# Sending the first two units of a feed-forward layer through half of the weights at a time

## The chip, the cores and the metric

The kernel runs on one core of a Trainium2 chip. The time is the device time of one execution in microseconds (us). Engines: TensorE (PE, with its weight loads as PEld), VectorE (DVE), ScalarE (ACT), GpSimd (POOL) and SyncE (SP), whose queue issues all DMAs here.

## What is computed

Causal attention over 8 batches, 8 heads, 576 tokens and 64 columns a head, blended with a read from a memory matrix, then a feed-forward layer over all 4608 tokens. Shortened:

```
scores = q @ k.T / 8, causal;  a = softmax(scores);  local = a @ v
q_p = elu(q) + 1
mem_out = (q_p @ M_prev) / (q_p @ z_prev + 1e-6)
attn = sigmoid(beta) * mem_out + (1 - sigmoid(beta)) * local      # [8, 8, 576, 64]
x = attn, heads side by side                                      # [4608, 512]
h = x @ w_in                                                      # w_in  [512, 2048], float64
out = (h * sigmoid(h)) @ w_out                                    # w_out [2048, 512], float64
```

## The kernel before

**Attention** goes head by head, 64 in all, batch by batch. `scores` makes one head's probabilities: transposes on VectorE (L221), score products on TensorE (L250), the row minimum on VectorE (L252), exponentials on ScalarE (L254), scaling on GpSimd (L304). `values` transposes the probabilities, multiplies by the values and writes the head's 64 columns into `xt` in two parts, the first 256 tokens and the other 320 (L425 or L430). The first ten heads ("whole") use plain float32 products; the later ones split each operand into a high and a low part in the faster format F32R. Two heads overlap: the scores of head n stand between the values of head n-1.

**Preparation of the weights.** Each of the 2048 ff columns belongs to one of 16 chunks of 128; a chunk has a tile of `w_in` ("i") and one of `w_out` ("o"), so 32 in all. They come as float64. `load_weight` (L138) brings a tile in as words, and `split_weight` makes float32 of it and then a high and a low part: three instructions on VectorE (L152, L154, L159), three on ScalarE (L150, L158, L161) and two on GpSimd (L156, L162). Twenty of the 32 stay in SBUF; twelve ("FLOW") are stored to DRAM and fetched again for each unit (L485).

**The feed-forward layer** works on 18 units of 256 tokens. `split_x` makes the high and low part of a unit's `xt` (L504, L505). A unit needs all eight heads of its batch: units 0 and 1 need heads 0 to 7, unit 2 needs heads 8 to 15. For each of the eight pairs of chunks p there are 24 first products (L552, into `h`), tanh and the blend (L563, L564), the split of g (L567 on ScalarE, L569 on GpSimd, or on VectorE once attention is over), and 12 second products (L532), which add up over all pairs in two PSUM tiles `acc`. The second product of pair p follows the first product of pair p+1. At the end of a unit `acc` is copied with scale 0.5 (L579) and stored (L581).

**Order.** A planner at the end of the function interleaves three generators: one step of attention, then as many weight tiles and product steps as are due. A head has ten steps, since its nine yields are followed by the call that ends it. Preparation is due at `PREP_RATE` = 3 tiles per nine steps, and `PREP_AFTER` = 3 after the first eight heads. Product steps begin when eight heads are done, at step 88; a unit has 17. The first 34 steps come at `FIRST_RATE` = 0.2 units per nine attention steps, later ones at `FFN_RATE` = 0.22. Where a unit's heads are not done, the planner goes on with attention. What attention leaves over runs at the end. The order of the text is a priority: the framework puts the instructions of each engine in order by it, and moves one up when it is ready and the engine would be idle.

Buffers that the parts share: "row" (4: `wy` of the preparation, `th`, `o`), "g" (4: raw weights and g), `xu` (6), one PSUM tile for `h` during attention, two for `acc`.

Of the kernel before, what the change touches and what calls it, by code (L numbers as in the profile page):

```python
# [8 lines left out]
F32 = mybir.dt.float32  # L9
# [3 lines left out]
AF = mybir.ActivationFunctionType  # L13
ALU = mybir.AluOpType
# [14 lines left out]
N_WHOLE = 10  # L29
ROW_BUFS = 4  # L30
W_AHEAD = 2
PREP_RATE = 3.0
PREP_AFTER = 3.0
FFN_RATE = 0.22
FIRST_RATE = 0.2
FIRST_UNITS = 2
W_EARLY = 2

# [2 lines left out]
def memory_attention_then_silu_ffn(ctx, tc, q, k, v, M_prev, z_prev, beta, w_in, w_out, out):  # L41
    nc = tc.nc
    B, H, S, D = q.shape
    NT, DM = out.shape
    DFF = w_in.shape[1]
    P = 128
# [4 lines left out]
    T = 256  # L51
    NU = NT // T
    KD = DM // P
    KF = DFF // P
    NP = KF // 2
# [5 lines left out]
    FLOW = {("i", c) for c in FLOW_IN} | {("o", c) for c in FLOW_OUT}  # L61
# [4 lines left out]
    dram = ctx.enter_context(tc.tile_pool(name="scratch", bufs=1, space=DRAM))  # L66
# [6 lines left out]
    def f(ap):  # L73
        return ap.bitcast(F32)
# [11 lines left out]
        out=mask[:, 3 * P:], in_=mask[:, 3 * P:], pattern=[[-1, P]], base=0, channel_multiplier=1,  # L86
# [54 lines left out]
    def split_weight(kind, c, raw):  # L141
# [24 lines left out]
    ready, anchor = set(), {}  # L166


    order = [
        (kind, 2 * x + j) for p in range(NP + 1) for kind, x in (("i", p), ("o", p - 1))  # L170
        if 0 <= x < NP for j in range(2)]
    loaded = []

    def load_next(n):
# [4 lines left out]
    def preparation():  # L179
        for n, x in enumerate(order):  # L180
            with tc.issue_after(anchor["dve"]):
                split_weight(*x, loaded.pop(0))
            load_next(n + W_AHEAD)
            ready.add(x)
            yield
# [248 lines left out]
    done = [0]  # L434
# [37 lines left out]
                second = values(b, h, made, xt[b, h // 2], n < N_WHOLE)  # L472


    flow_order = [(kind, 2 * p + j) for p in range(NP + 1) for kind, p in (("i", p), ("o", p - 1)) for j in range(2)]
    flow_order = [x for _ in range(NU) for x in flow_order if x in FLOW]
    flowing = []

    def flow():
        if flow_order:  # L480
            while flow_order[0] not in ready:
                yield "prepare"
            x = flow_order.pop(0)
            t = weight_tile(*x)
            nc.sync.dma_start(out=f(t), in_=scratch[x])  # L485
            flowing.append((x, t))

    def fetch(kind, c):
        if (kind, c) not in FLOW:
            return weight[kind, c]  # L490
        x, t = flowing.pop(0)
        assert x == (kind, c)
        return t

    def split_x(u):
        xu = []
        for kk in range(KD):
            t = pool.tile([P, 2, T], F32R, tag="xu", name="xu", bufs=XU_BUFS)
            t0 = u * T
            while t0 < (u + 1) * T:  # L500
                b = t0 // S
                n = min((b + 1) * S, (u + 1) * T) - t0
                src, o = xt[b, kk][:, t0 - b * S:t0 - b * S + n], t0 - u * T
                nc.scalar.copy(t[:, 0, o:o + n], src)  # L504
                nc.vector.tensor_tensor(out=t[:, 1, o:o + n], in0=src, in1=f(t[:, 0, o:o + n]), op=ALU.subtract)  # L505
                t0 += n
            xu.append(t)
        return xu

    def heads_needed(u):  # L510
        return ((u + 1) * T - 1) // S * H + H

    def ffn():
        ahead = None
        for _ in range(FLOW_BUFS):
            yield from flow()
        for u in range(NU):
            while done[0] < heads_needed(u):
                yield "wait"
            xu = ahead or split_x(u)  # L520
            ahead = None
            bank, tag = (ps_s, "s") if done[0] == B * H and u % 2 else (ps_a, "a")
            acc = [bank.tile([P, DM], F32, tag=tag, name="acc") for _ in range(T // P)]

            def second(p, g):
                for c in range(2):
                    w = fetch("o", 2 * p + c)
                    for t in range(T // P):
                        at = slice(t * P, (t + 1) * P)
                        terms = [(g[:, gi, c, at], w[:, wi]) for gi, wi in ((0, 0), (0, 1), (1, 0))]  # L530
                        for n, (ta, tb) in enumerate(terms):
                            nc.tensor.matmul(  # L532
                                acc[t], ta, tb, start=p == 0 and c == 0 and n == 0,
                                stop=p == NP - 1 and c == 1 and n == len(terms) - 1)
                    if ("o", 2 * p + c) in FLOW:
                        yield from flow()

            before = None
            for p in range(NP):
                while not {("i", 2 * p), ("i", 2 * p + 1)} <= ready:  # L540
                    yield "prepare"
                if done[0] == B * H and p % 2:
                    h = ps_t.tile([P, 2, T], F32, tag="t", name="h")
                else:
                    h = ps_h.tile([P, 2, T], F32, tag="h", name="h")
                for c in range(2):
                    w = fetch("i", 2 * p + c)
                    w4 = w.rearrange("p a (k f) -> p a k f", f=P)
                    for kk in range(KD):
                        terms = [(w4[:, wi, kk], xu[kk][:, xi]) for wi, xi in ((0, 0), (0, 1), (1, 0))]  # L550
                        for n, (ta, tb) in enumerate(terms):
                            nc.tensor.matmul(  # L552
                                h[:, c], ta, tb, start=kk == 0 and n == 0,
                                stop=kk == KD - 1 and n == len(terms) - 1)
                    if ("i", 2 * p + c) in FLOW:
                        yield from flow()
                yield
                if before:
                    yield from second(*before)

                h = h.rearrange("p c t -> p (c t)")
                th = pool.tile([P, 2 * T], F32, tag="row", name="th", bufs=ROW_BUFS)
                nc.scalar.activation(th, h, AF.Tanh, scale=0.5)  # L563
                nc.vector.scalar_tensor_tensor(out=th, in0=th, scalar=1.0, in1=h, op0=ALU.add, op1=ALU.mult)  # L564
                g = pool.tile([P, 2, 2, T], F32R, tag="g", name="g", bufs=G_BUFS)
                hi, lo = (g[:, j].rearrange("p c t -> p (c t)") for j in range(2))
                nc.scalar.copy(hi, th)  # L567
                late = nc.vector if done[0] == B * H else nc.gpsimd
                late.tensor_tensor(out=lo, in0=th, in1=f(hi), op=ALU.subtract)  # L569
                while not {("o", 2 * p), ("o", 2 * p + 1)} <= ready:  # L570
                    yield "prepare"
                before = p, g
                if p == NP - 2 and u + 1 < NU and done[0] >= heads_needed(u + 1):
                    ahead = split_x(u + 1)
                yield
            yield from second(*before)
            for t in range(T // P):
                o = pool.tile([P, DM], F32, tag="row", name="o", bufs=ROW_BUFS)
                nc.scalar.activation(o, acc[t], AF.Copy, scale=0.5)  # L579
                r0 = u * T + t * P  # L580
                nc.sync.dma_start(out=out[r0:r0 + P, :], in_=o)  # L581
            yield

    A_STEPS, F_STEPS = 9, 2 * NP + 1
    att, prep, prod = attention(), preparation(), ffn()
    steps, produced, steps_made = 0, 0.0, 0
    going = True
    while going:  # L590
        going = next(att, "end") != "end"
        steps += 1
        started = done[0] >= H
        while going and len(ready) < min(2 * KF, steps * (PREP_AFTER if started else PREP_RATE) / A_STEPS):
            next(prep)
        if started:
            produced += (FFN_RATE if steps_made >= FIRST_UNITS * F_STEPS else FIRST_RATE) * F_STEPS / A_STEPS
        while going and produced >= 1.0:
            said = next(prod, "end")
            if said == "wait":  # L600
                produced = min(produced, 1.0)
                break
            if said == "prepare":
                next(prep)
                continue
            produced -= 1.0
            steps_made += 1
# [28 lines left out]
```

## Time and profile before

| | |
|---|---|
| median of 3 runs | 1315.68 us (1314.75 to 1318.42) |
| the profiled execution | 1315.66 us, span 1313.9 us |
| PE busy / PEld busy | 1266.3 us (96%) / 1084.0 us (83%) |
| DVE / ACT / POOL busy | 898.1 us (68%) / 884.5 us (67%) / 822.9 us (63%) |
| chain that ended last, by engine | PE 73%, DVE 11%, ACT 6% |
| first products L552 | 2592 + 864 matmuls |
| second products L532 | 864 + 864 matmuls |

The profile is one execution. "Busy" is the time in which an engine has an instruction; TensorE's matmuls are pipelined, so a full PE isn't yet PE at its peak, and the weight loads (PEld) show better how densely it works. A row of a table of stretches gives the stretch, its length, then the busy time of each engine with the number of instructions in brackets, the granted clock of TensorE (1.00 is full speed), the busy share of the DMA engines and GB/s. Where the table is asked for one line or tile alone, it has only the columns of the engines that run it. A row of the order of time gives start and duration of an instruction, its engine, line, operation and tiles.

### The profile page before, as it was taken

To read this page: it belongs to the slowest core of one execution; us is meant where nothing else is said; L and a number is where in the kernel's file an instruction comes from. 1 tells how busy PE (TensorE), PEld (TensorE's weight loads), DVE (VectorE), ACT (ScalarE), POOL (GpSimd) and SP (SyncE) were. 2 spreads that over 40 slices of the span, in tenths; PEclk is the share of its full clock that TensorE was granted. 3 is DMA by queue.
4 is the path that set the end of the run, shared out by engine and by line. 5 is a ranking of instruction groups with operands and counts; after the bars stand their busy time and mean duration, and the time that the engine had idled before them with its cause. 6 is when DMAs were issued, how large, how long until landed. Compare 5 with 4: busy or idle time off the path is not lost.

```text
span 1313.9 us, 24653 instructions
## 1 busy us (share of the span) xinstructions
PE 1266.3 (96%) x7858; PEld 1084.0 (83%) x7858; DVE 898.1 (68%) x2472; ACT 884.5 (67%) x2143; POOL 822.9 (63%) x1133
## 2 busy tenths in 40 slices
PE   6988999999999999999999999999999999999998
PEld 2343458888999989998988989899898998999997
DVE  7988875778777777787767777777877775332222
ACT  6777866777787777777777777787878774322222
POOL 6878995777777777777777777767767763000000
PEclk9987779999999999999999999999999999999999
DMA  6766555555455555555555555555545432444444
GB/s 165 188 184 168 162 134 164 144 131 146 125 145 147 138 153 138 150 131 149 137 137 143 145 138 154 137 137 136 158 129 156 123 123 81 145 154 149 152 156 143
DMA packets 302994, 190.39 MB, mean 145 GB/s; under 512 B 258832, under 2 KB 267024, under 8 KB 302864
## 3 DMA queue, kind: packets, MB, share of 16 engines
q1 hardware_dynamic: 302864, 188.82, 51.9%
q8 instruction: 62, 1.02, 0.3%
q14 instruction: 68, 0.56, 0.1%
HBM read 173.02 MB, written 15.73 MB: 144 GB/s over the span
## 4 chain that ended last, share of the span: by engine, by line
PE 73%; DVE 11%; ACT 6%; issue 3%; POOL 3%; DMA 3%; SPq 1%; POOLq 0%; DVEq 0%; ACTq 0%
PE h L552 28%; PE acc L532 25%; PE x L422 7%; PE s L250 5%; PE tp L376 4%; PE tq L351 1%; PE x L414 1%; DVE s L252 1%; DVE wy L159 1%; DVE pl L407 1%; DVE st L290 1%; ACT p L254 1%; POOL p L304 1%; PE s L274 1%; DVE wy L154 1%
## 5 line engine op out<-in xcount | busy, mean ns | idle before, releaser
L552 PE MATMUL h<-xu,wi 128*128 128x256 f32 x2592 | 376.8, 287 | 8.7 <-DVE th L564 6.1
L552 PEld LDWEIGHTS h<-xu,wi 128*128 128x128 f32 x2592 | 343.0, 191 | 24.6 <-DVE th L564 7.8
L532 PE MATMUL acc<-wo,g 128*128 128x512 f32 x864 | 243.0, 398 | 0.0
L532 PE MATMUL acc<-flow,g 128*128 128x512 f32 x864 | 231.0, 394 | 0.5 <-DMA flow<-wo_s 0.5
L304 POOL TENSOR_SCALAR p<-p,st 128x384 f32<-128x384 f32 (+3 forms) x320 | 182.8, 592 | 75.3 <-DVE st L302 72.2
L564 DVE SCALAR_TENSOR_TENSOR th<-th,h 128x512 f32<-128x512 f32 x144 | 98.2, 683 | 143.5 <-ACT th L563 141.7
L532 PEld LDWEIGHTS acc<-flow,g 128*128 128x128 f32 x864 | 158.8, 188 | 33.6 <-DMA flow<-wo_s 1.0
L254 ACT ACTIVATE p<-s,st 128x128 f32<-128x128 f32 (+3 forms) x256 | 134.9, 528 | 69.9 <-DVE st L252 52.8
L569 POOL TENSOR_TENSOR g<-th,g 128x512 fp32r<-128x512 f32 x108 | 140.2, 1298 | 48.7 <-ACT g L567 46.9
L532 PEld LDWEIGHTS acc<-wo,g 128*128 128x128 f32 x864 | 149.1, 189 | 18.9 <-POOL p L304 0.5
L563 ACT ACTIVATE th<-h 128x512 f32<-128x512 f32 x144 | 85.9, 597 | 99.7 <-PE h L552 97.4
L407 DVE TENSOR_TENSOR pl<-tp,ph 128x384 fp32r<-128x384 f32 x216 | 118.5, 551 | 34.6 <-ACT ph L406 31.3
L252 DVE CUSTOM_DVE_ANT_0 s<-s,mask 128x128 f32<-128x128 f32 (+3 forms) x256 | 125.3, 491 | 23.1 <-PE s L250 19.6
L567 ACT CAST g<-th 128x512 fp32r<-128x512 f32 x144 | 89.2, 620 | 53.0 <-DVE th L564 52.1
L376 PE MATMUL tp<-ident,p 128*128 128x128 f32 x640 | 121.8, 291 | 3.2 <-POOL p L304 2.5
L552 PE MATMUL h<-xu,flow 128*128 128x256 f32 x864 | 122.6, 283 | 0.0
L406 ACT CAST ph<-tp 128x384 fp32r<-128x384 f32 x216 | 104.7, 490 | 26.1 <-PE x L422 21.2
L552 PEld LDWEIGHTS h<-xu,flow 128*128 128x128 f32 x864 | 112.8, 191 | 1.9 <-issue 0.3
L376 PEld LDWEIGHTS tp<-ident,p 128*128 128x128 f32 x640 | 82.2, 148 | 28.6 <-POOL p L304 9.0
L422 PE MATMUL x<-pl,vs 128*128 128x256 f32 x324 | 82.1, 308 | 0.9 <-DVE pl L407 0.9
L232 POOL TENSOR_TENSOR kk<-tt,kk 64x576 fp32r<-64x576 f32 x54 | 77.4, 1432 | 5.0 <-ACT kk L230 1.2
L422 PE MATMUL x<-ph,vs 128*128 128x320 f32 (+4 forms) x378 | 78.2, 275 | 1.4 <-POOL vs L316 0.8
(104 smaller groups left out, 2409.5 us busy)
## 6 DMA issues: line engine op xcount, KB each, us to landing
flow<-wo_s SPq DMA_DIRECT2D x144, 512.0 KB, 3.6
flow<-wi_s SPq DMA_DIRECT2D x72, 512.0 KB, 3.8
raw<-in_k SPq DMA_DIRECT2D x128, 72.0 KB, 2.5
raw<-in_q SPq DMA_DIRECT2D x128, 72.0 KB, 2.7
out<-o SPq DMA_DIRECT2D x36, 256.0 KB, 4.2
wraw<-in_moe_w_in SPq DMA_DIRECT2D x16, 512.0 KB, 4.4
qn<-in_q SPq DMA_DIRECT2D x64, 128.0 KB, 2.9
vr<-in_v SPq DMA_DIRECT2D x64, 128.0 KB, 2.5
```

The costliest lines, as they stand in the source:

```text
L252: anchor["dve"] = nc.vector.tensor_tensor_reduce(s, s, mask[:, 3 * P - P * i:], QS, 3.0e38, ALU.add, ALU.min, st[:, i:i + 1]).ins
L254: nc.scalar.activation(pt, s, AF.Exp, bias=st[:, i:i + 1], scale=-1.0, accum_out=st[:, 10 + i:11 + i])
L304: nc.gpsimd.tensor_scalar(pb[x], pb[x], st[:, 15 + x:16 + x], 1.0, op0=ALU.mult, op1=ALU.mult)
L376: nc.tensor.transpose(t[:, o:o + P], pb[i][:, P * j:P * j + P], ident)
L406: nc.scalar.copy(ph[:, 0:o], t[:, 0:o])
L407: nc.vector.tensor_tensor(out=pl[:, 0:cut], in0=t[:, 0:cut], in1=f(ph[:, 0:cut]), op=ALU.subtract)
L422: nc.tensor.matmul(x[0:rows, q0:n], vs[0:n_k, j], part[0:n_k, o:o + n - q0], start=False, stop=last)
L532: nc.tensor.matmul(acc[t], ta, tb, start=p == 0 and c == 0 and n == 0, stop=p == NP - 1 and c == 1 and n == len(terms) - 1)
L552: nc.tensor.matmul(h[:, c], ta, tb, start=kk == 0 and n == 0, stop=kk == KD - 1 and n == len(terms) - 1)
L564: nc.vector.scalar_tensor_tensor(out=th, in0=th, scalar=1.0, in1=h, op0=ALU.add, op1=ALU.mult)
L567: nc.scalar.copy(hi, th)
L569: late.tensor_tensor(out=lo, in0=th, in1=f(hi), op=ALU.subtract)
```

## The change

Units 0 and 1 no longer go through all eight pairs of chunks at once. There are four runs for them: unit 0 with pairs 0 to 3, unit 1 with pairs 0 to 3, unit 1 with pairs 4 to 7, unit 0 with pairs 4 to 7. A run of four pairs has nine product steps, so units 0 and 1 have 36. The first run of a unit stores its two scaled `acc` tiles to DRAM (`sums`), the second run loads them and adds them to its own. Unit 0's `xu` is made twice. The weight tiles are prepared in the order in which the runs use them, so that the first 16 serve pairs 0 to 3. The planner prepares 2 tiles per nine steps instead of 3, and 8 instead of 3 after the first eight heads; the first 34 product steps come at 0.6 instead of 0.2. The planner now counts its due tiles from where it stands, so that a tile made early on demand doesn't hold up the next.

```
-PREP_RATE = 3.0
-PREP_AFTER = 3.0
+PREP_RATE = 2.0
+PREP_AFTER = 8.0
 FFN_RATE = 0.22
-FIRST_RATE = 0.2
+FIRST_RATE = 0.6
...
+    runs = [(0, 0, NP // 2), (1, 0, NP // 2), (1, NP // 2, NP), (0, NP // 2, NP)]
+    runs += [(u, 0, NP) for u in range(2, NU)]
+    uses = [
+        (kind, 2 * x + j) for u, p0, p1 in runs for p in range(p0, p1 + 1)
+        for kind, x in (("i", p), ("o", p - 1)) if p0 <= x < p1 for j in range(2)]
+    order = sorted(set(uses), key=uses.index)
+    sums = [dram.tile([T // P, P, DM], F32, name=f"sum{u}") for u in range(2)]
...
-    flow_order = [x for _ in range(NU) for x in flow_order if x in FLOW]
+    flow_order = [x for x in uses if x in FLOW]
...
-        for u in range(NU):
+        for n_run, (u, p0, p1) in enumerate(runs):
             while done[0] < heads_needed(u):
                 yield "wait"
-            xu = ahead or split_x(u)
+            if n_run == 0 or runs[n_run - 1][0] != u:
+                xu = ahead or split_x(u)
             ahead = None
+            later = runs[n_run + 1][0] if n_run + 1 < len(runs) else u
...
-            for p in range(NP):
+            for p in range(p0, p1):
...
-                if p == NP - 2 and u + 1 < NU and done[0] >= heads_needed(u + 1):
-                    ahead = split_x(u + 1)
+                if p == p1 - 2 and later != u and done[0] >= heads_needed(later):
+                    ahead = split_x(later)
...
-                nc.scalar.activation(o, acc[t], AF.Copy, scale=0.5)
-                nc.sync.dma_start(out=out[r0:r0 + P, :], in_=o)
+                dest = out[r0:r0 + P, :] if p1 == NP else sums[u][t]
+                if p0:
+                    nc.sync.dma_start(out=o, in_=sums[u][t])
+                    nc.vector.scalar_tensor_tensor(
+                        out=o, in0=acc[t], scalar=0.5, in1=o, op0=ALU.mult, op1=ALU.add)
+                else:
+                    nc.scalar.activation(o, acc[t], AF.Copy, scale=0.5)
+                nc.sync.dma_start(out=dest, in_=o)
...
-        while going and len(ready) < min(2 * KF, steps * (PREP_AFTER if started else PREP_RATE) / A_STEPS):
+        while going and prepared < min(2 * KF, int(asked)):
             next(prep)
+            prepared += 1
+        asked = max(asked, prepared) + (PREP_AFTER if started else PREP_RATE) / A_STEPS
```

More of the change, by code (lines that the diff above doesn't have):

```diff
@@ L166, in memory_attention_then_silu_ffn @@
     ready, anchor = set(), {}
-    order = [
-        (kind, 2 * x + j) for p in range(NP + 1) for kind, x in (("i", p), ("o", p - 1))
-        if 0 <= x < NP for j in range(2)]
+    runs = [(0, 0, NP // 2), (1, 0, NP // 2), (1, NP // 2, NP), (0, NP // 2, NP)]
[5 more added lines that the diff above has]
+    sums = [dram.tile([T // P, P, DM], F32, name=f"sum{u}") for u in range(2)]
     loaded = []
@@ L472, in attention @@
                 second = values(b, h, made, xt[b, h // 2], n < N_WHOLE)
-    flow_order = [(kind, 2 * p + j) for p in range(NP + 1) for kind, p in (("i", p), ("o", p - 1)) for j in range(2)]
-    flow_order = [x for _ in range(NU) for x in flow_order if x in FLOW]
+    flow_order = [x for x in uses if x in FLOW]
     flowing = []
@@ L532, in second @@
                             nc.tensor.matmul(
-                                acc[t], ta, tb, start=p == 0 and c == 0 and n == 0,
-                                stop=p == NP - 1 and c == 1 and n == len(terms) - 1)
+                                acc[t], ta, tb, start=p == p0 and c == 0 and n == 0,
+                                stop=p == p1 - 1 and c == 1 and n == len(terms) - 1)
                     if ("o", 2 * p + c) in FLOW:
@@ L587, in memory_attention_then_silu_ffn @@
     att, prep, prod = attention(), preparation(), ffn()
-    steps, produced, steps_made = 0, 0.0, 0
+    asked, prepared, produced, steps_made = 0.0, 0, 0.0, 0
     going = True
@@ L591, in memory_attention_then_silu_ffn @@
         going = next(att, "end") != "end"
-        steps += 1
         started = done[0] >= H
-        while going and len(ready) < min(2 * KF, steps * (PREP_AFTER if started else PREP_RATE) / A_STEPS):
+        while going and prepared < min(2 * KF, int(asked)):
             next(prep)
+            prepared += 1
+        asked = max(asked, prepared) + (PREP_AFTER if started else PREP_RATE) / A_STEPS
         if started:
@@ L604, in memory_attention_then_silu_ffn @@
                 next(prep)
+                prepared += 1
                 continue
```

## The prediction

> **What bounds the kernel now.** I read the page's slices first, then one table of the span cut at the events that change the work (70, 174, 181, 318 us and the end of attention), then groups and single rows inside those stretches. The slices:
>
> ```profile
> span 1313.9 us, 24653 instructions
> PE   6988999999999999999999999999999999999998
> PEld 2343458888999989998988989899898998999997
> DVE  7988875778777777787767777777877775332222
> POOL 6878995777777777777777777767767763000000
> PEclk9987779999999999999999999999999999999999
> ```
>
> A slice is 33 us. From the seventh on TensorE is full at full clock: it is the bound, and its work is the same before and after. In the first five or six slices weight loads fill only 20 to 50%, VectorE and GpSimd are nearly full, and the granted clock sinks to 0.7. Time can be won in front of about 181 us and lost wherever TensorE is left without work later. The stretches (span, then PE, PEld, DVE, ACT, POOL, clock, DMA share, GB/s):
>
> ```profile
> 20.00:70.00 50.00, 47.16 (x108) 19.52 (x108) 43.36 (x105) 37.26 (x88) 42.50 (x39) 1.00 0.72 194
> 70.00:174.00 104.00, 89.34 (x271) 41.62 (x270) 94.09 (x208) 79.70 (x193) 90.46 (x81) 0.72 0.61 165
> 181.00:318.00 137.00, 135.13 (x875) 117.15 (x875) 98.25 (x278) 98.03 (x247) 97.20 (x137) 1.00 0.55 146
> 520.00:880.00 360.00, 353.75 (x2405) 325.21 (x2403) 266.73 (x791) 274.91 (x675) 262.37 (x384) 1.00 0.53 143
> 1133.00:1310.00 177.00, 176.48 (x1122) 159.83 (x1120) 48.05 (x76) 47.02 (x85) 0.00 (x0) 1.00 0.47 152
> ```
>
> From 70 to 174 us VectorE is busy 94.09 of 104 (90%), GpSimd 90.46 (87%), TensorE 89.34 (86%, at a clock of 0.72). From 181 to 318 us, where units 0 and 1 run, TensorE idles 2 us of 137.
>
> Why 174 and 318: the first product of a unit needs the columns of all eight heads of its batch. The single rows (start, duration):
>
> ```profile
> 169.96 0.36 ACT L425 COPY xt<-x 64x256 f32<-64x256 f32 x1
> 174.00 0.56 DVE L505 TENSOR_TENSOR xu<-xt,xu 128x256 fp32r<-128x256 f32 x1
> ...
> 314.49 0.43 DVE L430 TENSOR_TENSOR xt<-x,xb 64x256 f32<-64x256 f32 x1
> ...
> 317.47 0.98 DVE L505 TENSOR_TENSOR xu<-xt,xu 128x256 fp32r<-128x256 f32 x2
> ...
> 323.00 0.59 ACT L579 ACTIVATE o<-acc 128x512 f32<-128x512 f32 x1
> ```
>
> Head 7's first half lands at 170, unit 0's last split runs at 174; head 15's first half lands at 314, unit 2's last split at 317, and unit 1's result leaves at 323. So unit 2 has its input 5 us before unit 1 is out: the planner's 0.2 units per nine steps is just slow enough that TensorE is never without a unit. This is what the change disturbs.
>
> **What it costs in pieces.** For 70 to 174 us: the instructions on wy (three of VectorE and two of GpSimd for each weight chunk), and the copies L425 (two a head):
>
> ```profile
> 70.00:174.00 104.00, 50.58 (x58) 11.89 (x20) 54.00 (x38) 0.72 0.61 165
> 70.00:174.00 104.00, 4.68 (x12) 0.72 0.61 165
> ```
>
> x12 is 6 heads, 17.3 us each; a chunk takes VectorE 50.58/(58/3) = 2.62 us and GpSimd 54.00/(38/2) = 2.84 us; without chunks a head takes VectorE (94.09-50.58)/6 = 7.3 us and GpSimd 6.1 us. For the middle and the tail: L221 (one a head), L564 (eight a unit; middle, then tail), L505, L569:
>
> ```profile
> 520.00:880.00 360.00, 16.17 (x21) 1.00 0.53 143
> 520.00:880.00 360.00, 28.65 (x42) 1.00 0.53 143
> 1133.00:1310.00 177.00, 21.99 (x32) 1.00 0.47 152
> 520.00:880.00 360.00, 9.11 (x24) 1.00 0.53 143
> 520.00:880.00 360.00, 0.00 (x0) 55.68 (x43) 1.00 0.53 143
> ```
>
> The tail does 32/8 = 4 units in 177 us: 44.25 us of TensorE a unit. The middle does 42/8 = 5.25 units and 21 heads: 353.75 - 5.25 x 44.25 = 121.4, so 5.8 us of TensorE a split head. VectorE, less L564 and L505: (266.73-28.65-9.11)/21 = 10.9 us a head.
>
> **The change, part by part.** All planner positions are counted from the code: a head is ten steps (nine yields of scores and the call that ends it), and eight heads are done at step 88.
>
> *Fewer chunks early.* 2/9 instead of 3/9 a step: 19 chunks instead of 30 stand ahead of step 88, 2.22 instead of 3.33 a head. VectorE then needs 7.3 + 2.22 x 2.62 = 13.1 us a head against 7.3 + 3.22 x 2.62 = 15.7 measured (19.3 chunks in 6 heads): a sixth less, 17.3 becomes 14.4 if VectorE binds, 17 us over the 6 heads. TensorE has its own floor there: 89.34/6 = 14.9 us a head at the clock of 0.72; it can give 6 x (17.3-14.9) = 14.4 us, and nothing if the clock stays at 0.5. I take the floor at 0.72, the stretch's own clock: 14.4 us. From 20 to 70 us TensorE is busy 47.16 of 50, so at most 2.8 us more; I take it, since VectorE and GpSimd lose work there too. Together **-17.2** us, between 0 and -20. The Trainium skill ("TensorE: Matmul & The Clock Gate", Part 1: The HAM clock gate) says the array's clock is gated to half by default and that sustained activity releases it, so a denser TensorE would get more clock and VectorE's 17 us would be the limit. By that the total would be 3 us lower; the trace agrees only in part, for 86% busy got 0.72.
>
> *The thirteen chunks moved behind step 88.* They come in 15 steps, 8/9 a step, beside 1.5 heads and 17 of the 36 product steps of units 0 and 1 (0.94 unit, 7.6 pairs of chunks). TensorE: 0.94 x 44.25 + 1.5 x 14.9 x 0.72 (a whole head at full clock) = 57.7 us. GpSimd: 13 x 2.84 + 7.6 x 55.68/43 + 1.5 x 6.1 = 55.9 us. VectorE: 13 x 2.62 + 7.6 x 0.68 + 8 x 0.38 + 1.5 x 7.3 = 53 us. TensorE hides them only if GpSimd reaches 97%; at the 90% that the best engine of the early stretch reached, 55.9 becomes 62, **+4** us. Queued behind a late chunk on GpSimd is L569, which makes the low half of g, and the second product waits for that. The upper bound comes from where the last chunks meet unit 0 now:
>
> ```profile
> 180.00:200.00 20.00, 20.00 (x117) 14.24 (x116) 11.54 (x32) 14.11 (x34) 19.34 (x23) 0.99 0.66 169
> 220.00:240.00 20.00, 20.00 (x139) 18.41 (x138) 13.89 (x37) 13.51 (x32) 13.40 (x20) 1.00 0.42 114
> ```
>
> 117 matmuls in 20 us against 139, with GpSimd at 19.34: 16% fewer, 11 us on 58. The lower bound is 0.
>
> *Units 0 and 1 at 0.6.* 1.13 product steps a planner step: both units stand between step 88 and step 121, position (head 12, step 0). Unit 2 needs head 15, done at (16, 7); its first half, enough for the split, comes at about (16, 3). In between stand 4.3 heads of attention and no product at all; before, the products of units 0 and 1 reached to (17, 6). TensorE has 5.8 us of work a head there. With VectorE at the same 90% a head takes 10.9/0.905 = 12.0 us, and TensorE idles 4.3 x 6.2 = **+26.7** us. Bounds: VectorE full, 4.3 x 5.1 = 22; a head as slow as beside products, 360/21 = 17.1, 4.3 x 11.3 = 49. I take 26.7 since without products and chunks nothing holds VectorE below the share it reached in the early stretch. Unit 2 then starts alone, with no end of a unit to fill the wait for its first g: **+1**.
>
> *Halves and sums.* Two more changes of run, each ending in two copies of 0.59 us (L579) ahead of the next second product; TensorE has two first products of the next run, 24 matmuls each, in between, some 5.5 us (44.25/8), which hides them (1.2 us each otherwise). Four stores and four loads of 256 KB on SP's queue, ahead of the flow loads:
>
> ```profile
> out<-o SPq DMA_DIRECT2D x36, 256.0 KB, 4.2
> ```
>
> 4.2 us each and the additions end in about the same 5.5 us; four extra splits are 8 x 0.4 us on two engines with room. **0**, at most 3. Flow loads keep their number, twelve a unit.
>
> The sum: -17.2 + 4 + 26.7 + 1 = +14.5 us on the profiled execution's 1315.66 us (span 1313.9, 1.8 around it; the median of the runs is 1315.68): **1330.2 us**.
>
> **The rivals.** *The gap is filled (faster).* The order on each engine isn't strictly the planner's: work that is ready early moves up. A row of unit 0's first product and the transpose that begins head 5 for it, and two rows of unit 0's end against it:
>
> ```profile
> 67.40 0.52 PE L552 MATMUL h<-xu,wi 128*128 128x256 f32 x1
> ...
> 71.33 0.78 DVE L221 STREAM_TRANSPOSE tt<-raw 128x576 f32<-128x576 f32 x1
> ...
> 251.33 0.60 ACT L579 ACTIVATE o<-acc 128x512 f32<-128x512 f32 x1 [0.88 <-PE acc L532]
> 251.76 0.49 DVE L430 TENSOR_TENSOR xt<-x,xb 64x320 f32<-64x320 f32 x1
> ```
>
> A matmul that stands behind step 88 ran at 67 us, when head 5 of the eight had not begun. If attention of heads 12 to 15 moves up in the same way between the products of units 0 and 1, TensorE stays full, the gap costs nothing and the early gain stays: 1315.7 - 17.2 + 4 = 1302.5 us. It decides from about half: when over 2.3 of the 4.3 heads move up, the change is no longer slower. Against it: unit 0's results leave at 251 us together with head 11's second half, which is just where the planner has them ((13, 1) and (12, 8)), although every operand of unit 0 was there from 174 us. With TensorE full, the planner's order holds.
>
> *The early stretch gains nothing.* TensorE got a clock of 0.72 there on average; at 0.5, 14.9 us become 21.4 a head. If the clock follows the thinner products of the early heads and not the chunks, the -17.2 goes: 1347 us. For it: TensorE at 94% from 20 to 70 us. Against it: VectorE and GpSimd at 90 and 87%, half of that chunks.
>
> *The clock falls in the gap.* TensorE would be busy there 5.8 of 12.0 us a head. At a clock of 0.5 it needs 11.6; at the early stretch's share of 86% a head takes 13.5 us, 4.3 x 1.5 = 6 us more: 1337 us. The same section of the Trainium skill says that idle windows of about 3.4 us bring the half clock back. For it: the 0.72 at 86% busy; against it: 5.8 us come in short bursts all through a head.
>
> **How the numbers follow.** Forecast (a gap that costs 20 to 35 us) 0.50; gap filled by half or more 0.33; no early gain 0.08; clock falls 0.09. A measurement of this kernel tells about 0.3%, 4 us, from no change: faster means below 1311.7, slower above 1319.6. The filled gap ends faster in 0.26 and within the bound in 0.07; the forecast reaches the bound in 0.06 (early gain at 20 and gap at 22) and is slower otherwise. Faster 0.26, same 0.13, slower 0.61. The range 1303 to 1347 reaches from the filled gap to the missing early gain; the forecast's own is 1320 to 1342.
>
> **What would show it.** In the changed profile unit 0's last split should come at about 157 us instead of 174, with heads 14.9 us apart; the four runs should end by about 280 us; then some 50 us with TensorE near half busy, its matmuls those of attention alone, and unit 2's split at about 332 us instead of 317. From there all goes as now, 14 us later. A TensorE that stays above 95% from 160 us on makes the forecast wrong; so does a split of unit 0 later than 168 us, or a distance of heads in the gap under 9 us.

## The result, and the profile after

The changed kernel takes 1352.18 us (median of three executions) against 1315.22: 1.0272 times as long, 95% interval 1.0248 to 1.0296, so 37 us slower. A fourth execution of it took 4147.30 us; such slow ones are left out of every ratio here. 1330.2 was forecast, with 1347 as the upper end. The profiled execution took 1352.71 us. Its slices:

```profile
span 1350.9 us, 24607 instructions
PE   6999987899999999999999999999998999999998
PEld 2344466688899989888989998989897989999997
DVE  6697777767577877677777787777777766322222
POOL 6577797955677777777777777767676765000000
PEclk9777798899999999999999999999998999999999
```

A slice is 34 us. Of TensorE's row, slices six to eight (169 to 270 us) sink to 8, 7 and 8: that is where units 0 and 1 run, a stretch that was full before (9 in each of its slices). The same stretches as a table (length, then PE, PEld, DVE, ACT, POOL, clock, DMA, GB/s), first of the changed kernel:

```profile
70.00:157.00 87.00, 79.20 (x257) 34.67 (x255) 70.94 (x177) 64.64 (x162) 62.65 (x65) 0.76 0.54 146
157.00:282.00 125.00, 105.81 (x577) 86.12 (x578) 95.09 (x224) 89.54 (x210) 109.41 (x121) 0.88 0.58 165
282.00:320.00 38.00, 38.00 (x259) 35.23 (x258) 23.56 (x63) 22.02 (x56) 20.74 (x29) 1.00 0.61 174
320.00:337.00 17.00, 15.13 (x89) 13.67 (x88) 12.90 (x36) 11.67 (x30) 8.62 (x13) 0.90 0.58 179
337.00:1171.00 834.00, 807.99 (x5426) 739.93 (x5425) 609.79 (x1764) 602.53 (x1496) 575.88 (x843) 0.99 0.49 133
```

and of the kernel before, cut at the same events:

```profile
174.00:327.00 153.00, 150.38 (x957) 129.13 (x956) 109.67 (x303) 111.43 (x277) 112.19 (x155) 0.98 0.56 148
327.00:1133.00 806.00, 794.34 (x5393) 730.61 (x5391) 591.59 (x1747) 598.42 (x1480) 564.35 (x829) 1.00 0.51 138
```

The events are unit 0's last split (157 and 174 us), unit 2's first tanh (337 and 327) and the end of unit 13 (1171 and 1133); the cuts at 282 and 320 only divide the middle part. In the changed kernel the first two are these rows (start, duration; L436 is head 15's first half):

```profile
156.40 1.38 DVE L510 TENSOR_TENSOR xu<-xt,xu 128x256 fp32r<-128x256 f32 x3
...
331.58 0.42 DVE L436 TENSOR_TENSOR xt<-x,xb 64x256 f32<-64x256 f32 x1
...
333.73 0.34 DVE L510 TENSOR_TENSOR xu<-xt,xu 128x192 fp32r<-128x192 f32 x1
...
337.31 0.60 ACT L570 ACTIVATE th<-h 128x512 f32<-128x512 f32 x1 [0.24 <-PE h L559]
```

So three parts carry the whole difference of the spans, 1350.9 - 1313.9 = 37: unit 0's split comes 17 us **sooner** (157 against 174); from there to unit 2's first tanh it takes 181 us instead of 153, **+28**; from there to the end of the span 1014 us instead of 987, **+27**. The first is as forecast. The second was forecast as +32, but from other causes. The third was not forecast at all.

The rows say more on the second. TensorE idles 21 us in it instead of 3 (125 - 105.81 and 17 - 15.13, against 153 - 150.38), and the granted clock is 0.88 and 0.90 in two of its three rows, which takes 125 x 0.12 + 17 x 0.10 = 17 us of full clock away; the 0.98 before took 3. So half clock has nearly as large a share in the loss as idle time. The two stretches don't hold quite the same work either: in the middle stand 577 + 259 + 89 = 925 matmuls instead of 957, behind it 5426 instead of 5393. By an estimate at the 6.7 a us of the kernel before (5393 in 806 us) some 5 us of work have moved from the second part to the third, so that the losses themselves are nearer 33 and 22 us.

The second part from close by, in the changed kernel around 240 us (engine, line, operation):

```profile
233.05 4.63 PE L559 MATMUL h<-xu,wi 128*128 128x256 f32 x24 [1.48 <-DVE th L571]
...
233.99 0.61 ACT L574 CAST g<-th 128x512 fp32r<-128x512 f32 x1
...
234.79 0.83 POOL L241 TENSOR_TENSOR qq<-tt,qq 64x64 fp32r<-64x64 f32 x1
...
235.69 1.28 POOL L162 TENSOR_TENSOR flow<-wy,flow 128x512 fp32r<-128x512 f32 x1
...
237.69 1.42 POOL L238 TENSOR_TENSOR kk<-tt,kk 64x576 fp32r<-64x576 f32 x1
...
239.84 1.28 POOL L162 TENSOR_TENSOR flow<-wy,flow 128x512 fp32r<-128x512 f32 x1
...
241.08 1.27 POOL L576 TENSOR_TENSOR g<-th,g 128x512 fp32r<-128x512 f32 x1
...
242.08 0.58 ACT L570 ACTIVATE th<-h 128x512 f32<-128x512 f32 x1
...
245.18 0.69 DVE L571 SCALAR_TENSOR_TENSOR th<-th,h 128x512 f32<-128x512 f32 x1
...
245.93 1.70 PE L559 MATMUL h<-xu,wi 128*128 128x256 f32 x12 [0.99 <-DVE th L571]
```

The high half of g is ready at 234.6 us, and its low half starts at 241.08: GpSimd does two tiles' low halves and four pieces of attention first (two of them are shown). The next h is complete at 237.7 but gets its tanh at 242.08 and VectorE's blend at 245.18, 2.5 us after the tanh ended, and only then is the one PSUM tile of h free: TensorE's next first product starts at 245.93, 8.2 us behind the last one. No single wait is long; each link of the chain stands behind a moved tile or a head.

### The profile page after: what moved, and what is told of

It reads as the page before. It is cut to its first block, busy times and chain, and to the rows that moved or that the text cites. A ratio compares the mean times of both kernels' runs of the same rounds, so it can differ in the third digit from the quotient of the medians.

```text
span 1350.9 us, 24607 instructions
## 1 busy us (share of the span) xinstructions
PE 1277.1 (95%) x7858; PEld 1092.6 (81%) x7858; DVE 908.5 (67%) x2478; ACT 883.5 (65%) x2147; POOL 820.4 (61%) x1135
## 4 chain that ended last, share of the span: by engine, by line
PE 45%; DVE 3%; ACT 3%; POOL 2%; issue 1%; DMA 1%; SPq 0%; DVEq 0%; POOLq 0%; ACTq 0%
PE h L559 18%; PE acc L539 17%; PE x L428 3%; PE tp L382 2%; PE s L256 2%; POOL p L310 1%; DVE xu L510 1%; PE tq L357 1%; DMA flow<-wo_s 1%; PE x L420 1%; PE s L280 1%; ACT ph L412 0%; PE tp L399 0%; DVE s L258 0%; DVE th L571 0%
## 5 line engine op out<-in xcount | busy, mean ns | idle before, releaser
L559 PE MATMUL h<-xu,wi 128*128 128x256 f32 x2592 | 380.8, 292 | 20.1 <-DVE th L571 12.5
L559 PEld LDWEIGHTS h<-xu,wi 128*128 128x128 f32 x2592 | 350.2, 196 | 35.6 <-issue 8.4
L539 PE MATMUL acc<-flow,g 128*128 128x512 f32 x864 | 234.0, 398 | 0.8 <-DMA flow<-wo_s 0.8
L559 PE MATMUL h<-xu,flow 128*128 128x256 f32 x864 | 127.4, 289 | 1.7 <-DMA flow<-wi_s 1.7
L382 PEld LDWEIGHTS tp<-ident,p 128*128 128x128 f32 x640 | 79.4, 145 | 35.0 <-POOL p L310 9.5
L241 POOL TENSOR_TENSOR ql<-tt,qq 64x512 fp32r<-64x512 f32 x54 | 70.1, 1298 | 41.2 <-issue 20.6
```

The source lines that it names most:

```text
L382: nc.tensor.transpose(t[:, o:o + P], pb[i][:, P * j:P * j + P], ident)
L539: nc.tensor.matmul(acc[t], ta, tb, start=p == p0 and c == 0 and n == 0, stop=p == p1 - 1 and c == 1 and n == len(terms) - 1)
L559: nc.tensor.matmul(h[:, c], ta, tb, start=kk == 0 and n == 0, stop=kk == KD - 1 and n == len(terms) - 1)
```

## The experiments

Each kernel is placed by the same three lengths in its profile: unit 0's last split, from there to unit 2's first tanh, from there to the end of the span (us). late_no_gpsimd has no row: its profiled execution took 1359.40 us, 18 above its median.

| kernel | unit 0's split | to unit 2 | to the end |
|---|---|---|---|
| before | 174 | 153 | 987 |
| the change | 156 | 181 | 1014 |
| halves_only | 187 | 155 | 1003 |
| slow_first | 162 | 192 | 997 |
| prep_as_before | 173 | 167 | 1007 |
| spread | 158 | 186 | 1011 |
| planner_only | 175 | 153 | 995 |
| halves_no_sums | 178 | 155 | 993 |
| late_tiles_out | 154 | 164 | 1013 |
| hold_unit2 | 155 | 178 | 1019 |
| jitter_ffn | 176 | 153 | 988 |
| jitter_prep | 173 | 160 | 988 |
| low_on_vector | 155 | 182 | 1007 |
| first_06_alone | 172 | 164 | 1006 |
| later_slower | 166 | 178 | 1009 |
| middle | 162 | 169 | 1014 |

### The four parts of the change apart

The halves at the old rates:

```
 # the change with
-PREP_RATE, PREP_AFTER, FIRST_RATE = 2.0, 8.0, 0.6
+PREP_RATE, PREP_AFTER, FIRST_RATE = 3.0, 3.0, 0.2
```

> The four runs of units 0 and 1, the order of the weights and the sums in DRAM stay; the rates are those of before (3 tiles per nine steps throughout, first units at 0.2). Theory A (the tiles moved behind step 88 crowd VectorE and GpSimd beside the first products, and unit 2 begins a head too early in the plan): 1311 to 1320 us, unit 2's last split near 317 us as before. Theory B (the halves themselves cost: two more ends of runs, sums, a second split of unit 0): 1330 us or more. Theory C (the 0.6 rate and the gap behind it cost all): about 1315 us too.

1346.44 us, 1.0222 (1.0179 to 1.0264). My theory A failed here: the halves, with the planner's new counting, lose 32 us. But by the profile only 2 us of that lie where the halves run (155 against 153). 13 us lie ahead of unit 0, where nothing but the order differs, and 16 behind unit 2. The first of these shows in the clock of the early stretch (its rows from 60 and from 140 us):

```profile
60.00:80.00 20.00, 20.00 (x50) 9.47 (x50) 12.59 (x31) 12.39 (x31) 13.00 (x14) 0.50 0.44 118
...
140.00:160.00 20.00, 20.00 (x48) 8.61 (x47) 12.10 (x27) 11.69 (x31) 13.30 (x14) 0.50 0.42 111
```

TensorE is full at half clock while VectorE has 12 of 20 us to do. In the eight kernels with 2.9 or 3 tiles per nine steps the early stretch ended at 172 to 187 us. Three of them, halves_only, halves_no_sums and prep_as_before, have the same plan up to the first eight heads and end it at 187, 178 and 173, so a single profile's early time is uncertain by some 10 us.

The burst of tiles without the 0.6 rate, `FIRST_RATE = 0.2` in the change:

> The change with the first units at 0.2 again; weights at 2 and then 8 tiles per nine steps. Theory A: the early 17 us are won (unit 0's split at 157 us), but the thirteen tiles still come in about 1.5 heads and leave TensorE short of work there; unit 2's last split at 315 to 330 us, 1313 to 1328 us in all, and no further loss behind that, since unit 2 then begins at (18, x) of the plan. Theory C: the gap is gone and with it all the loss: 1298 to 1305 us. Theory B: 1340 us or more.

1354.42 us, 1.0312 (1.0266 to 1.0357). Theory C, the gap as the whole cause, is out: with no gap in the plan the middle part is the longest of all, 192 us. The burst and the lower rate ahead of it do that: with the old weight rates (halves_only) it is 155. Theory A's time failed too; unit 2's last split came at 349 us, where it had 315 to 330.

The 0.6 rate without the burst, `PREP_RATE = PREP_AFTER = 3.0` in the change:

> The change with the weights at 3 tiles per nine steps throughout; first units at 0.6. Theory A: unit 0's split at 174 us as before, units 0 and 1 out about 60 us sooner behind it than in the change, unit 2's last split at 317 to 330 us, then the same drift as in the change (about 20 us), since unit 2 still begins at (16, 7): 1333 to 1348 us. Theory C: a gap without products and TensorE half busy for 50 us; unit 2's split at 345 us, 1345 us or more. Theory B: 1340 us or more.

1351.83 us, 1.0274 (1.0246 to 1.0301). The middle is 167: 14 us over before, from the rate and the halves without any moved tiles. Theory A's time was 4 us too low. Unit 0's split and the 20 us behind unit 2 came as it said; but the four runs end at 310 us, 137 behind unit 0's split instead of the change's 172, so 35 us sooner and not 60, and unit 2's split came at 338 instead of 317 to 330. The time alone would fit theories B and C as well; the wait from the end of the runs to unit 2's split is 28 us, not C's 50.

The tiles moved, but not in a burst, `PREP_AFTER = 3.0, FIRST_RATE = 0.2` in the change:

> The halves with 2 tiles per nine steps before the first eight heads and 3 behind them, first units at 0.2: what the halves allow without a crowd of tiles. Theory A: unit 0's split at 157 us, unit 2's at 300 to 308 us, 1298 to 1306 us. Theory B: 1320 us or more. Theory C: 1298 to 1306 us.

1358.62 us, 1.0326 (1.0291 to 1.0361), the slowest, where theory A and C both saw a gain. Unit 0's split comes at 158 us, as hoped, and all of it and 17 us more are given back by unit 2: 186 us in the middle, where halves_only, which differs in the early rate alone, has 155. A moved tile costs its time beside the products, in a burst or not.

### What costs what

The planner's new counting alone, put into the kernel before:

```
-while going and len(ready) < min(2 * KF, steps * (PREP_AFTER if started else PREP_RATE) / A_STEPS):
+while going and prepared < min(2 * KF, int(asked)):
...
+asked = max(asked, prepared) + (PREP_AFTER if started else PREP_RATE) / A_STEPS
```

> The kernel before with nothing but the planner's new way of counting due tiles (the first tile comes two steps later, all else alike, no halves). Theory L (the early stretch hangs on TensorE's granted clock, and the order of its instructions shifts it either way): a change of a few us although no work changes, 1308 to 1335 us. Theory H (the loss of the halves at the old rates comes from the halves alone): 1313 to 1318 us.

1325.93 us, 1.0090 (1.0065 to 1.0116): 12 us from an edit that adds and removes no work. Theory L's time came true but not its place: the early stretch ends at 175 us against 174, and 8 of the profile's 9 us are lost behind unit 2. Nothing is lost up to unit 3's end; then comes this wait at the change to unit 4, with the stretch ahead of it, the stretch around it and a piece of that:

```profile
466.93 0.69 PE L250 MATMUL s<-kk,qq 128*128 128x384 f32 x1 [3.35 <-ACT p L254]
```

```profile
328.00:463.00 135.00, 132.55 (x899) 121.92 (x898) 99.47 (x298) 101.70 (x253) 98.97 (x145) 1.00 0.53 142
463.00:475.00 12.00, 8.65 (x46) 8.19 (x44) 8.94 (x24) 6.14 (x17) 6.79 (x11) 0.72 0.53 152
466.00:472.00 6.00, 5.07 (x23) 5.07 (x23) 5.20 (x13) 2.69 (x8) 2.49 (x4) 0.50 0.55 124
```

3.35 us of idle TensorE, and a granted clock of 0.50 from 466 to 472 us, 0.72 over the 12 us. The Trainium skill ("TensorE: Matmul & The Clock Gate", Part 1: The HAM clock gate) says that a window of about 3.4 us without activity halves the clock and that activity brings it back after another. The trace agrees in part: half clock follows here, and it ends, but the idle piece of 2.41 us shown further down was enough for it too. What such a wait costs can be estimated: 46 matmuls stand in the 12 us, at the 899 in 135 us ahead of it there would be 80, and the 34 that are missing are 5 us, one and a half times the wait.

The sums left out, in the kernel halves_only:

```
-dest = out[r0:r0 + P, :] if p1 == NP else sums[u][t]
-if p0:
...
 nc.scalar.activation(o, acc[t], AF.Copy, scale=0.5)
+if p1 < NP:
+    continue
+dest = out[r0:r0 + P, :]
```

> The halves at the rates of before, without the sums in DRAM: the first run of a unit stores nothing and the second adds nothing, so that half of each of the two units' sums is left out of the output. Theory S (stores and loads of the sums hold the four row tiles at the ends of runs and so delay the next tanh, some 4 us for each of the extra ends): 8 us less than the halves with the sums, 1330 to 1340 us. Theory H (order of the runs, not the sums): no change, 1337 to 1348 us.

1329.09 us, 1.0128 (1.0090 to 1.0166), 17 us under halves_only. That looks like theory S, but the profile denies it: the stretch in which sums are stored and loaded is 155 us with and without them, and the 18 us of the spans lie ahead of it and behind it, 9 and 9 us. The sums cost nothing that these profiles show.

The moved tiles' work left out of the change:

```
-split_weight(*x, loaded.pop(0))
+raw = loaded.pop(0)
+if n < 19:
+    split_weight(*x, raw)
+else:
...
+    nc.scalar.activation(t[:, j], raw.bitcast(U32)[:, 0:DM], AF.Copy, scale=2.0 ** -40)    # j = 0, 1
```

> The change with the work of the last 13 weight tiles left out on VectorE and GpSimd (each is filled by two casts on ScalarE from its raw words; those weights are not the right ones). Theory A (VectorE and GpSimd work of the moved tiles delays the chain from h to g and so TensorE): unit 0's split still at 157 us, the four runs done by about 290 us instead of 328, unit 2's split at 310 to 320 us, some 15 to 25 us less in all: 1327 to 1337 us. Theory G (the 0.6 rate puts attention of heads 12 to 15 behind the products, whatever the tiles cost): the runs are done sooner but unit 2's split stays at 325 to 335 us, and the time at 1345 to 1353 us.

1331.87 us, 1.0129 (1.0111 to 1.0146): 20 us under the change, 17 of the profile's in the middle part. (ScalarE does two instructions a tile here instead of three.) Its rows there, and behind:

```profile
154.00:282.00 128.00, 121.46 (x760) 102.70 (x761) 74.67 (x218) 93.16 (x225) 76.01 (x108) 0.99 0.69 199
282.00:298.00 16.00, 16.00 (x104) 14.46 (x103) 9.01 (x24) 10.25 (x25) 9.91 (x14) 1.00 0.65 193
298.00:318.00 20.00, 14.56 (x62) 11.19 (x60) 13.86 (x51) 13.18 (x37) 11.71 (x21) 0.66 0.39 95
318.00:1151.00 833.00, 811.52 (x5424) 743.11 (x5425) 614.23 (x1759) 603.02 (x1495) 576.93 (x841) 0.99 0.49 133
```

760 matmuls in the first 128 us against 577 in 125 with the tiles. And here stands the gap of the forecast: from 298 to 318 us 62 matmuls in 20 us at a clock of 0.66. It is 20 us long, not 52, and the middle part with it is 11 us over before, with 760 + 104 + 62 = 926 matmuls instead of 957. The four runs take 144 us from unit 0's split here and 172 in the change: the tiles' work delays them by 28 us, and 11 of these fill the time of the gap. Behind it nothing has got better: 1013 us. So the tiles' cost and the loss behind unit 2 are two things.

Two more experiments on the same cost: the low half of g on VectorE in units 0 and 1, and the moved tiles without GpSimd's part (the addition left out, the low half a cast on ScalarE):

```
-late = nc.vector if done[0] == B * H else nc.gpsimd
+late = nc.vector if done[0] == B * H or u < 2 else nc.gpsimd
```

> The change with the low half of g on VectorE instead of GpSimd in units 0 and 1 (16 instructions). Theory Q (the moved tiles delay the products since the low half of g waits in GpSimd's queue): the stretch from unit 0's split to unit 2's first tanh falls from 181 us to under 170, 1337 to 1345 us. Theory V (VectorE and the first tanh are as late as GpSimd; no single queue): within 5 us of the change, 1348 to 1357 us.

1348.95 us, 1.0272 (1.0220 to 1.0325): no change that can be told, and the middle part is 182 us. Theory V holds: to free the one step from GpSimd's queue doesn't help.

```
-nc.gpsimd.tensor_tensor(out=y, in0=y, in1=low, op=ALU.add)
-nc.gpsimd.tensor_tensor(out=t[:, 1], in0=w, in1=f(t[:, 0]), op=ALU.subtract)
+if early:
+    nc.gpsimd.tensor_tensor(out=y, in0=y, in1=low, op=ALU.add)
...
+if early:
+    nc.gpsimd.tensor_tensor(out=t[:, 1], in0=w, in1=f(t[:, 0]), op=ALU.subtract)
+else:
+    nc.scalar.copy(t[:, 1], w)
```

> The change without the GpSimd work of the last 13 tiles: the addition that completes the float32 value is left out, and the low half is a cast of the value on ScalarE instead of a difference; VectorE's three instructions stay. Theory Q: most of what leaving out all of it gave (20 us), 1332 to 1339 us. Theory V: half of it, 1339 to 1347 us.

1341.68 us, 1.0205 (1.0175 to 1.0235): about half of what leaving out all of it gave. So GpSimd's part of a tile makes about half of its cost, as theory V had it; that VectorE's part makes the other half was not measured by itself.

### The loss behind unit 2

Unit 2 held in the plan until 17 heads are done (`heads_needed(u) + (1 if u == 2 else 0)`):

> The change with unit 2 held in the plan until 17 heads are done instead of 16, so that it and all units behind it begin a head later, as they did before. Theory D (behind unit 2 the loss grows by 20 us since each unit begins in the plan just as its heads are done, and TensorE waits at each begin): unit 2's split at about 334 us still, but the growth behind it falls to under 8 us: 1336 to 1344 us. Otherwise: the growth stays, or a head more of gap is added: 1350 to 1360 us.

1356.20 us, 1.0330 (1.0292 to 1.0368). Theory D failed: it is 1019 us behind unit 2.

The 0.6 rate alone in the kernel before (`FIRST_RATE = 0.6`, whole units, no halves):

> The kernel before with the first units at 0.6 and nothing else: whole units, weights at 3 tiles per nine steps. Theory R (0.6 brings a gap in front of unit 2 and then waits of TensorE at the changes of units, whatever the halves): 10 to 20 us lost up to unit 2's first pair, and 12 to 25 us behind it (1000 us or more from there to the end instead of 987): 1335 to 1355 us. Theory K (the growth behind unit 2 comes with the four runs and their order): 987 to 995 us behind unit 2's first pair, 1322 to 1335 us in all.

1346.81 us, 1.0226 (1.0200 to 1.0252). Its middle and its end:

```profile
172.00:298.00 126.00, 124.10 (x790) 105.45 (x789) 74.28 (x199) 79.65 (x193) 81.05 (x104) 0.99 0.56 150
298.00:336.00 38.00, 29.40 (x148) 24.09 (x147) 29.13 (x92) 27.54 (x76) 23.34 (x38) 0.82 0.37 94
336.00:1162.00 826.00, 806.63 (x5423) 737.63 (x5422) 611.75 (x1760) 600.47 (x1495) 577.21 (x844) 0.99 0.50 135
```

The gap is here too (148 matmuls in 38 us; unit 1's results leave at 308), costs the same 11 us in the middle part, and 19 more are lost behind it. So theory R holds: one number, without halves or moved tiles, makes 11 of the 28 us and 19 of the 27.

The later units more slowly, `FFN_RATE = 0.205` in the change, and milder rates, `2.5, 4.0, 0.3`:

> The change with the later units at 0.205 instead of 0.22 per nine steps, so that attention runs ahead of them. If TensorE idles at changes of units since the heads of the next unit are late, the stretch behind unit 2's first pair falls from 1014 to under 1002 us: 1338 to 1346 us. If not, it stays at 1008 us or more: 1347 us or more.

1348.58 us, 1.0250 (1.0218 to 1.0281), 1009 us behind unit 2: attention run further ahead cures little.

> The halves with milder rates: weights at 2.5 and then 4 tiles per nine steps, first units at 0.3. By the costs so far: early gain 8 us; seven tiles moved, about 10 us; hardly a gap; behind unit 2 anything from 990 to 1010 us: 1322 to 1345 us, not faster than before.

1348.04 us, 1.0248 (1.0219 to 1.0278). That is 3 us over the range that was expected. The middle part is 169, with little burst and little gap; behind unit 2 it is 1014.

Two shifts of the kernel before that change no work, `FFN_RATE = 0.222` and `PREP_RATE = 2.9`:

> The kernel before with the later units at 0.222 instead of 0.22: a planner step shifts here and there behind unit 1, the work is the same. Theory T (the order of before is one that happens to keep TensorE fed at the begins of units; a shift loses some us there through gaps and half clock): 1318 to 1335 us, lost behind unit 2. Otherwise (the growth behind unit 2 belongs to the halves and the 0.6): 1313 to 1317 us.

1317.69 us, 1.0029 (1.0013 to 1.0046).

> The kernel before with 2.9 weight tiles per nine steps instead of 3 (one tile fewer before eight heads are done). Theory T: a few us to either side from the early stretch's clock and 5 to 20 us behind unit 2: 1318 to 1335 us. Otherwise: 1311 to 1317 us.

1322.38 us, 1.0062 (1.0042 to 1.0081). Both are slower, by 4 and 8 us, but not where theory T had it: both keep the 988 us behind unit 2, and 7 us of jitter_prep's profile are lost between unit 0's split and unit 2 (160 instead of 153).

What the 27 us consist of can be read from the rows of the first table: behind unit 2 TensorE idles 834 - 808.0 = 26 us instead of 806 - 794.3 = 12, and the clock is 0.99 instead of 1.00, at most some 8 us on 834; the 33 matmuls more are the other 5 by the estimate above. Most of the idle time stands within 8 us of a unit's end. One such piece, and the 7 us that follow at about half clock:

```profile
1029.27 0.49 DVE L336 TENSOR_REDUCE nrm<-r 128x5 f32<-128x320 f32 x1 [1.92 <-POOL r L334]
...
1031.69 0.41 PE L280 MATMUL s<-kk,qq 128*128 128x320 f32 x1 [2.41 <-DVE st L290]
...
1033.47 2.90 PE L559 MATMUL h<-xu,wi 128*128 128x256 f32 x12 [1.19 <-DVE th L571]
```

```profile
1033.00:1040.00 7.00, 6.53 (x33) 6.56 (x34) 4.24 (x12) 3.48 (x11) 4.24 (x6) 0.53 0.26 49
```

Here VectorE waited 1.92 us for a product of attention on GpSimd (L334), a score product waited 2.41 us for VectorE, and the next first products 1.19 us more for VectorE's blend. In the kernel before the clock reads 1.00 all through this part. What makes the changes of units worse in one order than in another was not found: not unit 2's place in the plan (hold_unit2), not attention's lead (later_slower), not the halves (first_06_alone). It doesn't need the 0.6 either: halves_only, slow_first and spread, at 0.2, lose 16, 10 and 24 us there. That stays open.

## Why the prediction was wrong

The direction was right and the size was not: +14.5 us forecast, +37 measured.

**Fewer chunks early, -17.2: right.** It is 17 us in the change, and seven kernels with this rate have unit 0's split at 154 to 166 us against 172 to 187 of eight with 2.9 or 3. The bound named was the right one too: from 70 to 157 us TensorE is busy 91% at a clock of 0.76, VectorE 82% and GpSimd 72%. The parts of the sum offset each other, though. Head 1's and head 7's first halves, the first row from the kernel before:

```profile
60.06 0.36 ACT L425 COPY xt<-x 64x256 f32<-64x256 f32 x1
```

```profile
52.74 0.36 ACT L431 COPY xt<-x 64x256 f32<-64x256 f32 x1
...
149.49 0.36 ACT L431 COPY xt<-x 64x256 f32<-64x256 f32 x1
```

Head 1 comes 7 us sooner, where 2.8 were forecast. Heads 2 to 7 come 16.1 us apart instead of 18.3 (14.9 instead of 17.3 was forecast), which is 13 us where 14.4 were forecast; and 3 us are lost again between head 7's half and unit 0's split (156.40, against 169.96 and 174.00 before). That the sum fits to 1 us is partly luck.

**The thirteen chunks behind step 88, +4, at most 11: wrong.** They cost 17 us of the profile (20 of the medians). The sum asked only whether each engine has the time; GpSimd's 109.41 of 125 us is indeed 88%, close to the 87% of the early stretch. What it left out is the chain from h to g: three engines in turn, each with tiles and heads in its queue, and one PSUM tile for h behind it. TensorE waits for the sum of these delays, pair by pair, and not for the fullest engine; so the rows around 240 us read, and to take one step from GpSimd's queue did not help (low_on_vector). I took 90% of one engine as the price of sharing; the row with 117 matmuls in 20 us was the better guide, although only four instructions of late tiles ran on GpSimd in it, two tiles' worth, and as an upper bound it was still too low.

**Units 0 and 1 at 0.6, +26.7: too high for the gap, and its mechanism half right.** The gap is there when the tiles are taken away, but costs 11 us (late_tiles_out, first_06_alone), half the lower bound of 22, or some 14 to 16 if the 31 and 19 matmuls that moved behind it are counted. Attention does move up between the products, as the rival of the filled gap had it: 4.3 heads in 52 us were forecast, and from the end of unit 1 or of the runs to unit 2's first tanh 28 and 20 us were seen. In the change itself the slow products left attention so much room that the gap all but vanished: the four runs end at 328 us, and head 15's half lands at 331.58.

**"From there all goes as now, 14 us later": the step that failed.** It was priced at nothing, and 27 us were lost behind unit 2, some 5 of them work that moved there. I read 354 busy of 360 us as a property of the work; it is a property of this order: with the same work TensorE idled 26 us instead of 12 and was granted half clock behind some of the waits. Why one order does that and another doesn't stays open. The forecast for unit 2's split (332 us) came out at 334, by luck: the tiles cost 13 us more than forecast and the gap 16 less.

**Halves and sums, 0: right where they run** (155 against 153 us).

Of the rivals, the clock in the gap came true in part (0.66 and 0.82 there), but its price is inside the 11 us.

## What to carry to other kernels

Where a pipeline has been brought to 98% of its bound by an order that a scheduler makes, every edit must be charged with a new order: a recount of due steps cost 12 us and a rate 30, with the same work, so run the scheduling part of a change alone before crediting or blaming the rest. Work moved beside a full engine is not hidden by free time on the other engines; follow the chain whose buffer that engine waits for, and add up the queues on it. An idle piece of 2.41 or 3.35 us of TensorE cost more than itself here, since the clock fell behind it.

## What was not expected of the hardware

The early stretch ran with TensorE 100% busy at a granted clock of 0.50 for 20 us at a time (halves_only, from 60 and from 140 us), while the kernel before was granted 0.72 on the average from 70 to 174 us; the end of this stretch moved by up to 15 us between kernels that have the same tiles in it. A full row of TensorE is thus no sign of full clock. The weight loads don't tell it either: they fill 9.47 of 20 us there and 9.28 in this row of the change, at a granted clock of 1.00 and with 87 matmuls instead of 50:

```profile
60.00:80.00 20.00, 19.70 (x87) 9.28 (x85) 15.60 (x43) 17.10 (x43) 14.97 (x18) 1.00 0.66 181
```

The column of the clock has to be read beside both.
